# Zeros and ones of the head set by GpSimd instead of VectorE, and another order of all engines: linear attention and softmax attention in one program on one core

## The chip, the core and the metric

The kernel runs on one NeuronCore of a Trainium2 chip. A core has five engines with instruction streams of their own: TensorE (PE, matrix products into PSUM), VectorE (DVE), ScalarE (ACT), GpSimd (POOL) and SyncE (SP, which here only issues DMAs). They meet at semaphores alone. The metric is the device time of one execution in microseconds, the median of several runs.

## What is computed

Two attention blocks of the same size (S = 2048, D = 512, 32 heads of 16 columns) with inputs of their own; the results stand side by side.

```python
def _A_ref(x, wqkv, wo):                      # linear attention
    q, k, v = ...                             # (x @ wqkv), 32 heads of Dh = 16
    phi = lambda t: jnp.where(t > 0, t + 1, jnp.exp(t)) + 1e-6
    pq, pk = phi(q), phi(k)
    kv = jnp.einsum("bhsd,bhse->bhde", pk, v)
    z = jnp.einsum("bhsd->bhd", pk)
    num = jnp.einsum("bhqd,bhde->bhqe", pq, kv)
    den = jnp.einsum("bhqd,bhd->bhq", pq, z)[..., None] + 1e-6
    return (num / den) @ wo                   # heads side by side
def _B_ref(x, wqkv, wo):                      # softmax attention
    scores = jnp.einsum("bhqd,bhkd->bhqk", q, k) * Dh ** -0.5
    p = _softmax(scores, axis=-1)
    return jnp.einsum("bhqk,bhkd->bhqd", p, v) @ wo
return jnp.concatenate([a, b], axis=-1)
```

## The kernel before

**The long work is block B's softmax.** A score block is 128 keys by 512 queries of one head (L923, 32 rows of the array, so that up to four blocks of different heads run side by side). There are 32 units (four groups of eight heads, four query chunks, even and odd heads), and each holds 64 blocks: 2048 in all. A block becomes exponentials in one of two ways. ScalarE reads two or three neighbouring score banks of pS and writes float16 into PT (L1135, 128x1024 or 128x1536, counted here as a two-block or three-block exponential); PT has 25 places. Or VectorE turns one bank (of pD, or the spare fifth bank of pS) into the bits of a float16 by a scaled conversion to int16 in DI (L1039), and GpSimd adds two constants to those bits (L1219), which gives two shifted copies; the weighted sum of the three stands for the exponential. In place of GpSimd, VectorE can do the two shifts itself (L1190), where the order says so. A block of ScalarE then costs TensorE one product with the values, pPV<-PT,VV (L1293), one of VectorE three, pPV<-DI,VX and twice pPV<-DI,VV.

**The end of a unit.** All products of a unit gather in one PSUM bank, pPV. When the last is done, VectorE transposes the bank (L1322), takes reciprocals of the sums (L1331) and writes the scaled rows to OT (L1327). Until L1327 has read it, no product of the next unit can start: the bank is closed.

**Beside it** run block B's projections (L630 and L729 into pD or pS, evicted by VectorE; L671 writes K rows to KR, from where DMAs spread them to KM), the whole of block A (L630 with xTa and Wa, L745 to L748 for phi, L795, L819, L831) and the output products (L630 and L1347, evicted at L616).

**The head** loads x and the weights, builds an identity matrix on VectorE (L504 to L511), transposes the third and fourth x tile on TensorE (L1426), copies them to xTb (L616: one by VectorE, one by ScalarE) and computes the first K and Q (L1438, evicted at L1448, L1450 and L1452), so that the first scores can start before the whole of x is there. In the same stretch VectorE sets the ones in VV (L536, L538), which make a column of sums, and the zeros of the second half of KM (L540, eight pieces), which is first read with the second group of heads. GpSimd sets identf, BMk and VNa's ones (L497 to L543).

**What sets the order.** Nothing is scheduled on the chip. While the program is built, a planner with a clock of its own picks the next instruction for each engine from those that are ready; a record of readers and writers adds the semaphores. Each row of the table SEG holds, from one planned time on (every 12 us), 27 numbers that the planner uses: how far VectorE and GpSimd may lag, how many products make a batch, how many banks a job may hold, ties and their random seed. Another table gives another order of the same work.

Of the kernel before, what the change touches and what calls it, by code (L numbers as in the profile page):

```python
# [238 lines left out]
def bass_concat_heads__linear_attn_block__softmax_full_mha__prompt_kernel(nc, A_x, A_wqkv, A_wo, B_x, B_wqkv, B_wo, out):  # L239
# [130 lines left out]
    sch = Sched()  # L370
    es = contextlib.ExitStack()
    with es:
# [14 lines left out]
        KM = sb("KM", [128, 2, 2, S], BF)  # L387
        VV = sb("VV", [128, 2, 4, 33 * 17], BF)
# [150 lines left out]
        for r_, e_, sc_ in zeros:  # L539
            sch.add("dve", lambda e, r_=r_, e_=e_, sc_=sc_: e.memset(KM[:, r_, e_, sc_ * 512:(sc_ + 1) * 512], 0.0), writes=km_keys(r_, e_, sc_))  # L540
# [1193 lines left out]
```

## Time and profile before

| | |
|---|---|
| median of 3 runs | 650.66 us (649.93 to 652.45) |
| the profiled execution | 650.58 us, span 648.7 us |
| first exponential starts | 10.33 us |
| last exponential ends | 640.90 us |
| granted TensorE clock, mean | 0.997 |

The profiled execution is 0.08 us under the median. In the rows of the trace, a group has its line, engine, operation, tiles (written <- read), shapes and count; then its busy time, the mean of one in ns, and the idle time of the engine just before with what ended it. A row of the timeline begins with start and duration in us and may hold several instructions (xcount). A row of a stretch (from:to) has its length, then busy time and instructions of PE, PEld (weight loads), DVE, ACT and POOL, the granted clock as a share of full speed, the share of the DMA engines and GB/s. A row of the waits tells who waited for whom: us in total, times, longest.

### The profile page before, as it was taken

The page shows a single profiled execution, that of the slowest core. Times are in us where ns is not written, and L with a number is a line of the kernel's source. Part 1 is how long each engine was busy: PE and PEld are TensorE (multiplying, and loading weights), DVE is VectorE, ACT ScalarE, POOL GpSimd, SP SyncE. Part 2 cuts the span into 40 slices and gives each one's busy share as a digit, 9 for nine tenths or more (in the row PEclk, how much of TensorE's full clock was granted, in tenths as well). Part 3 has the DMA queues.
Part 4 walks back from the last instruction along what each step waited for, and adds up shares of the span by engine and source line. Part 5 has one row for each costly group of instructions (what it writes and reads, how often), then busy time and mean ns, then how long its engine had stood idle before and what let it go on. Part 6 is the DMA issues. An engine that isn't in the chain of part 4 may idle for free.

```text
span 648.7 us, 19621 instructions
## 1 busy us (share of the span) xinstructions
PE 634.6 (98%) x8366; PEld 214.4 (33%) x8366; DVE 608.7 (94%) x1090; ACT 632.1 (97%) x688; POOL 430.3 (66%) x729
## 2 busy tenths in 40 slices
PE   7999999999999999999999999999999999999996
PEld 5333333333333333333333232323222232222222
DVE  7999999999999999999999999999989999988984
ACT  5999999999999999999999999999999999999995
POOL 1566777877677776667767667666777766665552
PEclk9999999999999999999999999999999999999999
DMA  9700200011010000101130111002100001101111
GB/s 210 180 3 2 42 2 18 2 42 35 2 31 6 1 11 9 36 18 35 35 82 18 35 26 27 17 8 52 43 10 18 2 11 42 41 2 42 50 43 53
DMA packets 53227, 21.75 MB, mean 34 GB/s; under 512 B 44176, under 2 KB 52624, under 8 KB 53136
## 3 DMA queue, kind: packets, MB, share of 16 engines
q1 hardware_dynamic: 51664, 19.80, 13.1%
q8 instruction: 67, 1.10, 0.7%
q10 hardware_dynamic: 1472, 0.66, 0.4%
q14 instruction: 24, 0.20, 0.1%
HBM read 4.46 MB, written 4.19 MB: 13 GB/s over the span
## 4 chain that ended last, share of the span: by engine, by line
PE 49%; ACT 41%; DVE 8%; DMA 1%; issue 1%; DVEq 0%
ACT PT L1135 40%; PE pPV L1293 19%; PE pS L923 17%; PE pD L630 5%; DVE DI L1039 4%; PE pS L630 3%; ACT EA L745 1%; PE pD L729 1%; PE pD L923 1%; PE pS L729 1%; DMA KNa<-VNa 1%; DVE pPV L1322 1%; PE pS L686 1%; DVE KNa L616 0%; DVE VNa L835 0%
## 5 line engine op out<-in xcount | busy, mean ns | idle before, releaser
L1135 ACT ACTIVATE PT<-pS 128x1024 f16<-128x1024 f32 (+1 forms) x650 | 619.2, 1105 | 4.7 <-PE pS L923 3.4
L1219 POOL INT64_ADD DI<-DI x716 | 428.1, 611 | 204.1 <-DVE DI L1039 201.8
L1039 DVE TENSOR_SCALAR DI<-pD 128x512 int16<-128x512 f32 x499 | 328.7, 681 | 19.3 <-PE pD L923 14.3
L923 PE MATMUL pS<-QT,KM 32*128 32x512 bf16 x1547 | 262.6, 385 | 4.2 <-ACT PT L1135 3.5
L1293 PE MATMUL pPV<-PT,VV 128*17 128x512 f16 x1333 | 236.6, 381 | 0.0
L1293 PE MATMUL pPV<-DI,VV 128*17 128x512 f16 x1430 | 228.7, 382 | 0.0
L923 PE MATMUL pD<-QT,KM 32*128 32x512 bf16 x501 | 175.6, 385 | 0.4 <-DVE VNa L835 0.2
L1293 PE MATMUL pPV<-DI,VX 128*17 128x512 f16 x715 | 164.0, 383 | 0.3 <-DVE OT L1327 0.3
L1039 DVE TENSOR_SCALAR DI<-pS 128x512 int16<-128x512 f32 x214 | 144.9, 677 | 1.6 <-PE pS L923 1.4
L923 PEld LDWEIGHTS pS<-QT,KM 32*128 32x128 bf16 x1547 | 66.9, 91 | 238.5 <-ACT PT L1135 189.5
L1293 PEld LDWEIGHTS pPV<-PT,VV 128*17 128x17 bf16 x1333 | 52.4, 88 | 45.3 <-issue 36.9
L1293 PEld LDWEIGHTS pPV<-DI,VV 128*17 128x17 bf16 x1430 | 51.7, 88 | 42.8 <-issue 27.9
L1293 PEld LDWEIGHTS pPV<-DI,VX 128*17 128x17 bf16 x715 | 36.3, 89 | 21.5 <-issue 14.5
L923 PEld LDWEIGHTS pD<-QT,KM 32*128 32x128 bf16 x501 | 42.0, 91 | 4.0 <-DVE DI L1039 1.3
L630 PE MATMUL pD<-Wa,xTa 128*32 128x256 bf16 x704 | 28.6, 275 | 0.4 <-DVE DI L1039 0.4
L630 PE MATMUL pD<-xTb,Wb 128*32 128x512 bf16 x336 | 27.0, 384 | 0.0
L1322 DVE STREAM_TRANSPOSE pPV<-pPV 128x512 f32<-128x512 f32 x31 | 22.3, 720 | 0.0
L630 PEld LDWEIGHTS pD<-Wa,xTa 128*32 128x32 bf16 x704 | 14.9, 95 | 11.0 <-issue 6.6
L630 PE MATMUL pD<-xTa,Wa 128*32 128x512 bf16 x192 | 15.7, 384 | 0.3 <-DVE DI L1039 0.2
L616 DVE CAST KNa<-pD 128x512 bf16<-128x512 f32 x20 | 13.6, 682 | 2.3 <-PE pD L630 1.8
L745 ACT ACTIVATE EA<-pD 128x512 bf16<-128x512 f32 x24 | 15.8, 659 | 0.0
L630 PE MATMUL pD<-Wa,KNa 128*32 128x512 bf16 x176 | 14.1, 390 | 0.8 <-DMA KNa<-VNa 0.7
(136 smaller groups left out, 341.4 us busy)
## 6 DMA issues: line engine op xcount, KB each, us to landing
out_dram<-KNa SPq DMA_DIRECT2D x31, 128.0 KB, 1.7
Wa<-in_A_wqkv_dram SPq DMA_DIRECT2D x1, 1536.0 KB, 8.4
KM<-KR SPq DMA_DIRECT2D x96, 16.0 KB, 1.8
Wb<-in_B_wqkv_dram SPq DMA_DIRECT2D x2, 384.0 KB, 5.1
Wb<-in_B_wqkv_dram SPq DMA_DIRECT2D x1, 512.0 KB, 4.8
Wa<-in_A_wo_dram SPq DMA_DIRECT2D x1, 512.0 KB, 3.9
Wa<-in_B_wo_dram SPq DMA_DIRECT2D x1, 512.0 KB, 3.8
ON<-in_B_x_dram ACTq DMA_DIRECT2D x1, 256.0 KB, 2.8
```

Of the source, the lines that this page charges most:

```text
L616: return lambda e, bk: (e.tensor_copy(out_fn(), in_fn(bk)) if lane == "dve" else e.activation(out_fn(), in_fn(bk), ACTF.Copy))
L630: ins = self.e.matmul(out_[32 * g:32 * g + 32], lhsT=lhsT[:, 32 * g:32 * g + 32], rhs=rhs, start=start, stop=stop, tile_position=(0, 32 * g))
L686: return e.matmul(f32v(bk)[:, tl * 128:(tl + 1) * 128], lhsT=xTb[:, cc, t * 128:(t + 1) * 128], rhs=xTb[:, cc, t * 128:(t + 1) * 128], sta ...
L729: return e.matmul(f32v(bk)[:, tl * 128:(tl + 1) * 128], lhsT=xTb[:, cc, t * 128:(t + 1) * 128], rhs=Wb[:, cc, 1024 + Gp * 128:1024 + Gp * ...
L745: ("act", 0.0635 + n * 0.000833, f_ev("act", lambda e, bk: e.activation(EA[:, 0:n], f32v(bk)[:, c0:c0 + n], ACTF.Exp), [], ["EA"])),
L923: return e.matmul(dst, lhsT=KM[32 * g:32 * g + 32, Gp % 2, e_, j * 128:(j + 1) * 128], rhs=QT[32 * g:32 * g + 32, Gp % 2, c * 512:(c + 1) ...
L1039: sch.add("dve", lambda e: e.tensor_scalar(DI[:, di_at(0, buf) + i * 512:di_at(0, buf) + (i + n) * 512], f32v(DBANK[b0], n * 512), ESC, EB ...
L1135: sch.add("act", lambda e: e.activation(PTf[:, p0 * 512:p0 * 512 + w], S5[:, c0:c0 + w], ACTF.Exp, scale=SC), reads=skeys(sl, len(bl)), wr ...
L1219: sch.add("pool", lambda e, v=v, word=word: e.int64_add(at64(v), at64(0), word), reads=keys, writes=[("DI", v, x) for x in best])
L1293: sch.add("pe", lambda e, g=g, j=j, c0=c0, V_=V_, r2=r2, P=P, first=first, last_=last_: e.matmul(PVb[32 * g:32 * g + 17, 0:512], lhsT=V_[: ...
L1322: sch.add("dve", lambda e: e.transpose(PVb[:, 0:512], PVb[:, 0:512]), reads=[("PV", g) for g in range(4)], writes=[("PV", g) for g in rang ...
```

## The change

There are two edits. Four memsets of VV and eight of KM move from VectorE's stream to GpSimd's, at the same place of the program, and all 54 rows but one of SEG have other numbers. The table comes from a search that keeps six partial orders and counts stretches with idle TensorE. The work is the same but for the split of the blocks: 627 two-block and 24 three-block exponentials on ScalarE instead of 617 and 33 (1326 blocks, before 1333), and 722 blocks instead of 715 on VectorE; four shifts are done by VectorE (L1190), before none.

```diff
     SEG = (
-        (0.0,0.15,4,3.0,0,0,6,2,10.0,26,2.5,7.0,1.2,2.5,2,7.0,1.5,2.5,1.5,3,1,0.3,6,0,-9.0,4,1,80),
+        (0.0,0.15,4,3.0,0,0,6,4,8.0,26,3.0,7.0,0.5,2.5,2,7.0,3.0,3,1.5,1,1,0.3,4,0,0.0,4,0.5,32),
...
-        (636.0,0.3,4,3,0,1,6,4,10.0,26,2.5,7.0,0.5,1.8,2,5.0,2.0,3,1.0,2,1,1.0,6,0,-9.0,4,0,82),
+        (636.0,0.2,5,3.0,4,1,6,2,8.0,36,3.5,9.0,0.8,1.8,2,7.0,1.5,2.5,1.0,2,1,0.3,4,10,-9.0,4,2,167),
     )
...
         for r_ in range(2):
-            sch.add("dve", lambda e, r_=r_: e.memset(
+            sch.add("pool", lambda e, r_=r_: e.memset(
                 VV[:, r_, :, :].rearrange("p t (h c) -> p t h c", c=17)[:, :, :, 16:17], 1.0), writes=[("VV1", r_)])
-            sch.add("dve", lambda e, r_=r_: e.memset(VV[:, r_, :, 544:560], 1.0), writes=[("VV1", r_)])
+            sch.add("pool", lambda e, r_=r_: e.memset(VV[:, r_, :, 544:560], 1.0), writes=[("VV1", r_)])
         for r_, e_, sc_ in zeros:
-            sch.add("dve", lambda e, r_=r_, e_=e_, sc_=sc_: e.memset(KM[:, r_, e_, sc_ * 512:(sc_ + 1) * 512], 0.0), writes=km_keys(r_, e_, sc_))
+            sch.add("pool", lambda e, r_=r_, e_=e_, sc_=sc_: e.memset(KM[:, r_, e_, sc_ * 512:(sc_ + 1) * 512], 0.0), writes=km_keys(r_, e_, sc_))
```

The first place is the head. On VectorE, the twelve memsets stood between the reduction for PAR and the copy of an x tile to xTb; as zeros of two bytes they were issued there as half as many words of four.

```order
 L515 MEMSET pPV 128x512
 L532 TENSOR_REDUCE PAR<-ZMk 128x1 x2
-L536 MEMSET VV 128x132
-L538 MEMSET VV 128x4x16
-L536 MEMSET VV 128x132
-L538 MEMSET VV 128x4x16
-L540 MEMSET KM 128x256 x8
 L616 COPY xTb<-pS 128x4x128
 L1448 TENSOR_SCALAR KM<-pS,PAR 128x128 x2
```

On GpSimd they now stand between the memset of EA and that of identf, and with 512 columns each.

```order
 L503 ISA DI<-DI 128x16
 L530 MEMSET EA 128x16
+L536 MEMSET VV 128x132
+L538 MEMSET VV 128x4x16
+L536 MEMSET VV 128x132
+L538 MEMSET VV 128x4x16
+L540 MEMSET KM 128x512 x8
 L497 MEMSET identf 128x128
 L498 AFFINE_SELECT identf<-identf 128x128
```

So VectorE's copy to xTb follows PAR at once, and GpSimd's identf, BMk and VNa come twelve instructions later.

The second place is the end of the 13th unit on VectorE, from the transpose of pPV on. Before, four instructions stand between it (L1322) and the reciprocal (L1331):

```order
L1322 STREAM_TRANSPOSE pPV<-pPV 128x512 [waits s_pe]
L1039 TENSOR_SCALAR DI<-pD 128x512
L1039 TENSOR_SCALAR DI<-pD 128x512 [waits s_pe]
L788 CAST VNa<-pS 128x4x128 [waits s_pe]
L1039 TENSOR_SCALAR DI<-pD 128x512 [waits s_pe]
L1331 RECIPROCAL ZR<-pPV 128x16
L1327 TENSOR_TENSOR OT<-pPV,ZR 128x8x2x16 [waits s_dve]
L1039 TENSOR_SCALAR DI<-pS 128x512 [waits s_pe]
L1039 TENSOR_SCALAR DI<-pD 128x512 [waits s_pe]
L1039 TENSOR_SCALAR DI<-pS 128x512 [waits s_pe]
L746 TENSOR_SCALAR EC<-EA 128x33x16 [waits s_act]
L748 SCALAR_TENSOR_TENSOR KNa<-pD,EC 128x512 [waits s_dve]
```

Now there are twelve; the transpose and the first two of them, conversions of pS and pD, stand just ahead of these rows:

```order
L671 CAST KR<-pD 128x512 [waits s_pe]
L1039 TENSOR_SCALAR DI<-pS 128x512 [waits s_pe]
L1039 TENSOR_SCALAR DI<-pD 128x512 [waits s_pe]
L659 CAST QT<-pD 128x512 [waits s_pe]
L1039 TENSOR_SCALAR DI<-pS 128x512 [waits s_pe]
L1039 TENSOR_SCALAR DI<-pD 128x512 [waits s_pe]
L659 CAST QT<-pD 128x512 [waits s_pe]
L1039 TENSOR_SCALAR DI<-pS 128x512 [waits s_pe]
L1039 TENSOR_SCALAR DI<-pD 128x512 [waits s_pe]
L671 CAST KR<-pD 128x512 [waits s_pe]
L1331 RECIPROCAL ZR<-pPV 128x16
L1327 TENSOR_TENSOR OT<-pPV,ZR 128x8x2x16 [waits s_dve]
```

Four evictions of projections (KR twice, QT twice) and eight conversions have come between. On TensorE, the same closing of the bank before; a run of pS<-QT,KM that waits for s_act fills score banks for ScalarE, and pPV<-PT,VV after s_dve is the first product of the next unit:

```order
L630 MATMUL pD<-Wa,xTa 32x256 [waits s_d11,s_dve]
L630 MATMUL pD<-Wa,xTa 32x256 x15
L923 MATMUL pS<-QT,KM 128x512 [waits s_act]
L923 MATMUL pS<-QT,KM 128x512
L923 MATMUL pS<-QT,KM 128x512 [waits s_dve]
L630 MATMUL pD<-Wa,xTa 32x256 x8
L923 MATMUL pS<-QT,KM 128x512 [waits s_act]
L923 MATMUL pS<-QT,KM 128x512
L923 MATMUL pD<-QT,KM 128x512 [waits s_dve]
L630 MATMUL pD<-Wa,xTa 32x256 x8
L1293 MATMUL pPV<-PT,VV 17x512 [waits s_dve]
L1293 MATMUL pPV<-DI,VX 17x512 x3
```

And now, from the last score group ahead of that first product on:

```order
L923 MATMUL pS<-QT,KM 128x512 [waits s_act]
L923 MATMUL pS<-QT,KM 128x512
L923 MATMUL pD<-QT,KM 128x512 [waits s_dve]
L630 MATMUL pD<-xTb,Wb 32x512 x8
L630 MATMUL pS<-Wa,xTa 32x256 [waits s_d11,s_dve]
L630 MATMUL pS<-Wa,xTa 32x256 x31
L630 MATMUL pD<-Wa,xTa 32x256 [waits s_dve]
L630 MATMUL pD<-Wa,xTa 32x256 x31
L1293 MATMUL pPV<-DI,VX 17x512 [waits s_dve]
L1293 MATMUL pPV<-DI,VX 17x512
L1293 MATMUL pPV<-PT,VV 17x512 x2
L1293 MATMUL pPV<-DI,VV 17x512
```

Two runs of 32 projection matmuls of block A (of 256 columns), and the rest of a K projection, now stand between one score group and the next, and ahead of the products of the next unit.

The third place is the end of TensorE's order. Before, after the last product of an exponential:

```order
L1293 MATMUL pPV<-PT,VV 17x512 [waits s_act]
L1293 MATMUL pPV<-PT,VV 17x512
L1347 MATMUL pS<-Wa,ON 128x512 x6
L1347 MATMUL pD<-Wa,xTb 128x512 [waits s_dve]
L1347 MATMUL pD<-Wa,xTb 128x512
L1347 MATMUL pS<-Wa,xTb 128x512 [waits s_dve]
L1347 MATMUL pS<-Wa,xTb 128x512
```

And now:

```order
L1293 MATMUL pPV<-PT,VV 17x512 [waits s_act]
L1293 MATMUL pPV<-PT,VV 17x512 x2
L1347 MATMUL pS<-Wa,ON 128x512
L1347 MATMUL pD<-Wa,ON 128x512 x3
L1347 MATMUL pS<-Wa,ON 128x512 x5
L1347 MATMUL pD<-Wa,xTb 128x512 [waits s_dve]
L1347 MATMUL pD<-Wa,xTb 128x512
L1347 MATMUL pS<-Wa,xTb 128x512 [waits s_dve]
L1347 MATMUL pS<-Wa,xTb 128x512
```

Nine output products instead of six stand between the last value product and the four that wait for VectorE's last transposes; the three others stood ahead of the last score group before.

102 rows, old and new, of the table SEG are left out of this document.

## The prediction

> **What bounds the kernel now.** I read the page first, then the stretches before, between and after the exponentials, ScalarE's waits, the groups by shape, and the timeline of the head and of the longest waits.
>
> ```profile
> PE 634.6 (98%) x8366; PEld 214.4 (33%) x8366; DVE 608.7 (94%) x1090; ACT 632.1 (97%) x688; POOL 430.3 (66%) x729
> ```
> ```profile
> 0.00:10.33 10.33, 7.81 (x71) 6.82 (x71) 7.64 (x38) 2.47 (x4) 2.11 (x13) 1.00 0.87 192
> 10.33:640.90 630.57, 623.93 (x8285) 206.66 (x8283) 597.92 (x1043) 628.53 (x682) 428.14 (x716) 1.00 0.13 30
> ```
> ```profile
> PEld pS L923 <- ACT PT L1135: 189.5, 482, 1.1
> ACT PT L1135 <- PE pS L923: 3.4, 2, 2.7
> ```
>
> In the long middle ScalarE is busy 628.53 of 630.57 us. TensorE's score matmuls stand 482 times waiting for a score bank that ScalarE has yet to read, and ScalarE waits for TensorE in rows twice. So ScalarE is the bound: the time is the start of its first exponential (10.33), its work, its waits, and a tail of 7.8 us (640.90 to 648.70).
>
> A busy row of ScalarE also holds waits, because rows overlap. The real pitch is the distance between starts:
>
> ```profile
> 565.29 5.67 ACT L1135 ACTIVATE PT<-pS 128x1024 f16<-128x1024 f32 x6
> 570.72 0.73 ACT L745 ACTIVATE EA<-pS 128x512 bf16<-128x512 f32 x1
> 571.20 7.11 ACT L1135 ACTIVATE PT<-pS 128x1024 f16<-128x1024 f32 x7
> ```
> ```profile
> L1135 ACT ACTIVATE PT<-pS 128x1024 f16<-128x1024 f32 x617 | 579.9, 1084 | 2.0 <-PE pD L923 0.9 <-PE pS L923 0.7
> L1135 ACT ACTIVATE PT<-pS 128x1536 f16<-128x1536 f32 x33 | 49.3, 1494 | 2.7 <-PE pS L923 2.7
> L1039 DVE TENSOR_SCALAR DI<-pD 128x512 int16<-128x512 f32 x497 | 326.3, 679 | 17.8 <-PE pD L923 12.8 <-PE pS L923 2.1
> L746 DVE TENSOR_SCALAR EC<-EA 128x528 bf16<-128x528 bf16 x32 | 13.4, 420 | 0.8 <-ACT EA L745 0.4
> ```
>
> Six two-block exponentials take 5.43 us, 0.905 each; an EA takes 0.48. A three-block one is longer by the difference of the means (1.494 - 1.084), so 1.315. That gives 617 x 0.905 + 33 x 1.315 + 32 x 0.48 = 617.2 us of work; the other 13.4 us of the middle are ScalarE's waits, most of them of some tens of ns. Two are large:
>
> ```profile
> 464.31:467.72 3.41, 2.73 (x25) 0.80 (x25) 3.41 (x6) 3.41 (x4) 2.21 (x5) 1.00 0.16 33
> 467.72:471.13 3.41, 3.41 (x29) 0.68 (x30) 2.49 (x6) 2.49 (x3) 2.00 (x4) 0.50 0.17 49
> ```
> ```profile
> 471.15 3.04 ACT L1135 ACTIVATE PT<-pS 128x1024 f16<-128x1024 f32 x3 [0.91 <-PE pD L923]
> 594.02 0.40 PE L630 MATMUL pD<-Wa,KNa 128*32 128x512 bf16 x4 [0.67 <-DMA KNa<-VNa]
> 594.78 1.94 ACT L1135 ACTIVATE PT<-pS 128x1024 f16<-128x1024 f32 x2 [0.71 <-PE pS L923]
> ```
>
> From 464.31 TensorE has only 25 matmuls in 3.41 us, because the pPV bank is closed while VectorE finishes a unit late. The granted clock is then 0.50 for 3.41 us, and ScalarE stands 0.91 plus two short waits, about 1.3 in all. At 594 a late transposed load costs 0.71.
>
> **The change, part by part.** First the head.
>
> ```profile
> 4.23 1.06 PE L1426 MATMUL pS<-identb,ON 128*128 128x128 bf16 x8
> 5.94 1.30 PE L1438 MATMUL pS<-xTb,Wb 128*128 128x128 bf16 x8
> 6.09 2.19 DVE L540 MEMSET KM<- 128x256 uint32 x8
> 8.19 0.36 DVE L616 COPY xTb<-pS 128x512 bf16<-128x512 bf16 x1
> 8.70 0.60 PE L1438 MATMUL pS<-xTb,Wb 128*128 128x256 bf16 x4 [1.46 <-DVE xTb L616]
> 9.34 0.43 DVE L1452 CAST QT<-pS 128x256 bf16<-128x256 f32 x1 [0.27 <-PE pS L1438]
> 9.89 0.60 PE L923 MATMUL pS<-QT,KM 32*128 32x512 bf16 x5
> 10.33 12.38 ACT L1135 ACTIVATE PT<-pS 128x1536 f16<-128x1536 f32 x12 [2.67 <-PE pS L923]
> ```
> ```profile
> 1.23 0.11 POOL L530 MEMSET EA<- 128x16 bf16 x1
> 3.28 0.29 DVE L511 TENSOR_SCALAR identb<-identf,IC 128x128 bf16<-128x128 f32 x1
> 4.23 0.20 POOL L525 MEMSET BMk<- 128x128 bf16 x1
> 18.36 1.20 POOL L1219 INT64_ADD DI<-DI  x2 [12.92 <-DVE DI L1039]
> 5.81 0.59 SPq L454 DMA_DIRECT2D Wb<-in_B_wqkv_dram  x1
> 12.16 0.62 PE L729 MATMUL pD<-Wb,xTb 128*128 128x128 bf16 x8
> Wb<-in_B_wqkv_dram SPq DMA_DIRECT2D x1, 512.0 KB, 4.8
> ```
>
> The transposes of the third and fourth x tile end at 5.29, but VectorE copies one of them only at 8.19, behind its memsets. The second Q matmuls wait for that copy (1.46). Without the memsets the copy stands behind PAR and is done by 6 us. The matmuls then follow the first Q group, whose last row ends at 5.94 + 1.30 = 7.24, and as the next row starts before one ends (four of them take 0.60), at 7.1 instead of 8.70. What follows (cast, scores, exponential) shifts with it: **-1.6 us**, the first exponential at 8.7. Behind it the next loads hold: the V weights land at 5.81 + 4.8 = 10.6, and their user moves from 12.16 to 10.56.
>
> GpSimd's price: 16 columns took 0.11, 128 took 0.20, so 512 take about 0.5; eight of them and four small ones are 5 us. Bounds: 2.7 (VectorE's 0.27 for the same bytes) and 9 us (four times the 0.20, and 1 us for each strided one). From 1.34 on that ends near 6.5, and the rest of its head near 8.5; its first shift is due at 18.36 - 1.6. Nothing waits; if the cover were gone, the upper bound would still end by 13. No DMA moves.
>
> **ScalarE's work.** There are 627 two-block and 24 three-block exponentials now: +10 x 0.905 - 9 x 1.315 = **-2.8 us**. The seven score blocks that left go to VectorE, at 0.6 each (two starts, below), beside two wide and two narrow shifts (L1190, bounded by half and twice L746's 0.42, 1.2 for the four): 5.4 us more for VectorE, and 14 more pPV matmuls (four at a time, 0.8 us) for TensorE. VectorE has 32.7 idle us in the middle, so most is covered; its lateness reaches ScalarE through a bank that comes free later. Bounds 0 and 5.4; I take **+0.5**, near the lower end, since L1039's own idle time (17.8) is a wait for TensorE.
>
> **The order.** What counts is whether TensorE has the next scores in time.
>
> ```profile
> 466.49 0.39 PE L923 MATMUL pS<-QT,KM 32*128 32x512 bf16 x3
> 466.81 0.83 PE L630 MATMUL pD<-Wa,KNa 128*32 128x512 bf16 x12
> 639.02 0.39 PE L923 MATMUL pS<-QT,KM 32*128 32x512 bf16 x2
> 619.40 21.50 ACT L1135 ACTIVATE PT<-pS 128x1536 f16<-128x1536 f32 x20
> 266.16 1.26 DVE L1039 TENSOR_SCALAR DI<-pD 128x512 int16<-128x512 f32 x2
> 267.34 0.68 DVE L788 CAST VNa<-pS 128x512 bf16<-128x512 f32 x1
> ```
>
> One place of the new order is worse than any of the old. At the end of the 13th unit VectorE has twelve instructions between the transpose of pPV and its reciprocal (four before): 12 x 0.6 = 7 us of closed bank. TensorE issues eight score groups without a pPV matmul, and after the last one eight projection matmuls, two runs of 32 with 256 columns, and eight pPV matmuls before the next scores. Its time: 0.32 to the first projection (466.49 to 466.81), 2 rounds of 0.22 (three rounds of four take 0.83, one 0.39), 16 half rounds of 0.11, and for the pPV run 0.32 + 0.22 again: 3.1 us. Its scores reach ScalarE 0.42 later (594.36 to 594.78), at 3.5. By then ScalarE has run dry: the last score group here is issued at 639.02 and its exponential ends at 640.90, so 1.7 after the issue the next could start. **+1.8 us**; bounds 0.9 (the runs overlap better) and 2.8 (VectorE's chain a microsecond behind).
>
> Against that the two large waits of before: their order is gone. Counted in rounds of 0.21 us, the four score groups there hold 7 rounds of TensorE's work, the emptiest four of the new order 9 (as some of the old order that kept their clock), so I take the clock's loss away, **-1.3**; bounds -1.3 and +1.4 (the same elsewhere). The late load I keep by half, since in the new order one such use stands four score groups behind its source: **-0.4**; bounds -0.7 and +0.7.
>
> Of the clock, TensorE: Matmul & The Clock Gate (Trainium skill, the two states) says that it halves after at least one idle window of about 3.4 us. The rows agree in the 3.41 us but not in the idleness: TensorE was busy 2.73 of 3.41. By the rule no stretch of either order would be slowed, and the sum would stay at -3.7; by the row a thinly filled stretch is enough, and the sum with one such loss would be -1.0 (+1.4 for -1.3).
>
> **The tail.** Nine output matmuls stand before the last pair, six before:
>
> ```profile
> 641.27 1.47 PE L1347 MATMUL pS<-Wa,ON 128*128 128x512 bf16 x6
> 643.06 0.60 PE L1347 MATMUL pD<-Wa,xTb 128*128 128x512 bf16 x2 [0.31 <-DVE xTb L1396]
> ```
>
> Three more at 0.21 fill the 0.31 and 0.1 to 0.2 more: **+0.1**.
>
> Sum: -1.6 - 2.8 + 0.5 + 1.8 - 1.3 - 0.4 + 0.1 = -3.7. The profiled execution took 650.58 (span 648.70 and 1.88 around it), 0.08 under the median of 650.66, so the forecast is 646.9.
>
> **Rivals.** *ScalarE never runs dry (better).* The long run of projections is hidden and neither large wait comes back: -1.6 - 2.8 - 1.3 - 0.7 = -6.4, so 644.2. For it: two old units had nine instructions at that place of VectorE's order, and neither is among the large waits. Against: the old order nowhere has the 3.1 us of work found here between two score groups.
>
> *The clock halves again*, once or twice at 1.3 to 1.4: 648.2 to 649.6. For it: the row at 467.72. Against: fuller runs.
>
> *GpSimd's memsets hold up VectorE's identity chain.* If each waits for the other, identb ends not at 3.57 but when GpSimd is through, up to 8 us; with the transposes (1.06), the first K and Q (1.30) and 1.63 from the second Q to the exponential that is 12.3 at the latest, 3.6 later than forecast: 650.5. Against: L746, from SBUF to SBUF, takes 0.42 in all its rows with GpSimd at work two thirds of the time. SBUF — State Buffer (Trainium skill, who interferes with whom) says that VectorE in a two-port mode and GpSimd lock each other out for a whole instruction; no row here shows it.
>
> *VectorE becomes the bound (slower).* If in the middle its 5.4 us are not covered, they come on top of an unchanged middle: +5.4 - 1.6 = +3.8, so 654.4. It decides where less than 5 of its 32.7 idle us can be used. For it: 94% busy. Against: its idle rows are waits for TensorE.
>
> *The order does not shift the middle*: what ScalarE saves is lost in new short waits, 649.
>
> **Numbers.** As summed 0.50 (645.2 to 648.6), better 0.19, clock 0.13, memsets 0.07, unchanged middle 0.05, VectorE 0.06. 0.5% (3.3 us) is about what a measurement of this kernel can tell from no change: faster is below 647.4. Of the first case 0.33 lies there, with the second 0.52; slower is the VectorE case, 0.06; the rest, 0.42, is the same. The range 643.4 to 650.4 leaves out VectorE's case and the ends.
>
> **What would show it.** The first exponential near 8.7; the GpSimd memsets near 0.5 each and ended by 7; 651 exponentials; a row of ScalarE idle for 1 to 2 us near 265 to 275, behind a run of L630; granted clock 1.00 throughout. The forecast is wrong if the head does not move, if VectorE's wait for TensorE vanishes, or if 0.50 stands in the clock again.

## The result, and the profile after

The changed kernel took 645.97 us (median of 5 runs, 645.90 to 646.66) beside 652.45 for the kernel before on the same chip (5 runs, 649.93 to 653.30): a ratio of 0.9912, interval 0.9888 to 0.9936. In two later comparisons, on two chips, it was 0.9946 (0.9927 to 0.9966) and 0.9919 (0.9897 to 0.9942). So it is faster by 0.5 to 0.9%. The forecast was 646.9 (643.4 to 650.4). The profiled execution took 645.92, its span is 644.19; before it was 650.58 and 648.75.

The busy times, and below them the stretches before the first exponential, between the first and the end of the last, and behind it (columns as before: length, then busy us and instructions of TensorE, its weight loads, VectorE, ScalarE and GpSimd, then clock and transfers):

```profile
PE 632.2 (98%) x8380; PEld 213.4 (33%) x8380; DVE 613.7 (95%) x1088; ACT 628.5 (98%) x689; POOL 438.7 (68%) x745
```
```profile
0.00:9.19 9.19, 6.56 (x71) 5.75 (x71) 7.42 (x26) 2.47 (x4) 7.47 (x25) 1.00 0.82 186
9.19:635.97 626.78, 622.26 (x8295) 206.35 (x8293) 603.21 (x1053) 624.97 (x683) 431.23 (x720) 1.00 0.14 31
635.97:644.20 8.23, 3.36 (x18) 1.28 (x16) 3.10 (x10) 1.09 (x2) 0.00 (x0) 0.90 0.23 71
```

The head went from 10.33 to 9.19 (-1.14), the middle from 630.57 to 626.78 (-3.79), the tail, taken to the last instruction, from 7.85 to 8.22 (+0.37): -4.56 of span. The 630.57 us of the middle held 597.92 us of VectorE work, so VectorE stood idle for 32.65; now it is 603.21 of 626.78, idle 23.57. VectorE does 5.3 us more and the stretch is 3.8 us shorter.

The exponentials by shape, which are the counts that the forecast took:

```profile
L1135 ACT ACTIVATE PT<-pS 128x1024 f16<-128x1024 f32 x627 | 586.5, 1083 | 1.5 <-PE pD L923 1.0 <-PE pS L923 0.3
L1135 ACT ACTIVATE PT<-pS 128x1536 f16<-128x1536 f32 x24 | 36.1, 1505 | 1.0 <-PE pS L923 1.0
```

The head on the timeline, first VectorE's first five identity rows before, then the rows after:

```profile
1.06 0.98 DVE L506 TENSOR_SCALAR identf<-identf 128x1 f32<-128x1 f32 x5
```
```profile
1.06 2.87 DVE L506 TENSOR_SCALAR identf<-identf 128x1 f32<-128x1 f32 x5
1.27 0.66 POOL L536 MEMSET VV<- 128x132 bf16 x1
2.88 3.99 POOL L540 MEMSET KM<- 128x512 bf16 x8
5.49 0.45 DVE L511 TENSOR_SCALAR identb<-identf,IC 128x128 bf16<-128x128 f32 x1
6.00 0.62 PE L1426 MATMUL pS<-identb,ON 128*128 128x128 bf16 x8 [1.57 <-DVE identb L511]
6.85 0.40 DVE L616 COPY xTb<-pS 128x512 bf16<-128x512 bf16 x1
6.90 1.26 PE L1438 MATMUL pS<-xTb,Wb 128*128 128x128 bf16 x12
9.19 4.62 ACT L1135 ACTIVATE PT<-pS 128x1536 f16<-128x1536 f32 x4 [1.05 <-PE pS L923]
```

Two things happened at once. VectorE's copy of the x tile no longer stands behind its memsets (8.19 before, 6.85 now). But the identity is ready only at 5.94 instead of 3.57: with GpSimd's memsets running from 1.27 to 6.87, the same five short VectorE instructions take 2.87 instead of 0.98, and TensorE stands idle for 1.57 us.

And the end of the 13th unit, where the forecast saw a new wait:

```profile
264.70 6.52 ACT L1135 ACTIVATE PT<-pS 128x1024 f16<-128x1024 f32 x7 [0.35 <-PE pS L923]
270.48 1.05 PE L630 MATMUL pS<-Wa,xTa 128*32 128x256 bf16 x32
271.35 1.05 PE L630 MATMUL pD<-Wa,xTa 128*32 128x256 bf16 x32
271.58 0.60 ACT L745 ACTIVATE EA<-pS 128x512 bf16<-128x512 f32 x1 [0.35 <-PE pS L630]
271.66 0.46 DVE L1327 TENSOR_TENSOR OT<-pPV,ZR 128x256 bf16<-128x256 f32 x1
272.22 0.38 PE L1293 MATMUL pPV<-DI,VX 128*17 128x512 f16 x2
273.19 7.45 ACT L1135 ACTIVATE PT<-pS 128x1024 f16<-128x1024 f32 x8 [1.02 <-PE pD L923]
```

ScalarE stands idle for 0.35, 0.35 and 1.02, together 1.72. The first of these waits (264.70) is ahead of the two runs of L630 with 32 matmuls, the other two (1.37) are behind them. The second run ends at 272.22 by its pace (0.87 a run), just when VectorE's multiply (to 272.12) has opened the pPV bank. Which of the two sets the wait these rows can't say.

### The profile page after: what moved, and what is told of

The parts are those of the page before. It is cut to its first block, busy times and chain, and to the rows that moved or that the text cites. A ratio compares the mean times of both kernels' runs of the same rounds, so it can differ in the third digit from the quotient of the medians.

```text
span 644.2 us, 19658 instructions
## 1 busy us (share of the span) xinstructions
PE 632.2 (98%) x8380; PEld 213.4 (33%) x8380; DVE 613.7 (95%) x1088; ACT 628.5 (98%) x689; POOL 438.7 (68%) x745
## 4 chain that ended last, share of the span: by engine, by line
ACT 48%; PE 43%; DVE 9%; issue 0%; DVEq 0%
ACT PT L1135 47%; PE pPV L1293 15%; PE pS L923 14%; PE pD L630 7%; DVE DI L1039 5%; PE pS L630 2%; ACT EA L745 1%; PE pD L729 1%; PE pD L923 1%; PE pS L729 1%; DVE identf L506 1%; DVE PQT L748 0%; DVE pPV L1322 0%; DVE VV L733 0%; PE pD L1347 0%; DVE VX L736 0%
## 5 line engine op out<-in xcount | busy, mean ns | idle before, releaser
L1039 DVE TENSOR_SCALAR DI<-pD 128x512 int16<-128x512 f32 (+1 forms) x491 | 324.0, 684 | 13.0 <-PE pD L923 9.7
L1293 PE MATMUL pPV<-DI,VV 128*17 128x512 f16 x1444 | 235.5, 381 | 0.0
L1293 PE MATMUL pPV<-DI,VX 128*17 128x512 f16 x722 | 166.1, 382 | 0.0
L1039 DVE TENSOR_SCALAR DI<-pS 128x512 int16<-128x512 f32 x228 | 154.6, 678 | 1.0 <-PE pS L923 0.5
L630 PE MATMUL pD<-Wa,xTa 128*32 128x256 bf16 x800 | 32.1, 275 | 0.1
L630 PE MATMUL pD<-xTb,Wb 128*32 128x512 bf16 x336 | 26.6, 384 | 0.5 <-DVE DI L1039 0.5
L1322 DVE STREAM_TRANSPOSE pPV<-pPV 128x512 f32<-128x512 f32 x31 | 22.3, 721 | 0.1
L630 PEld LDWEIGHTS pD<-Wa,xTa 128*32 128x32 bf16 x800 | 17.5, 96 | 11.0 <-issue 7.0
L616 DVE CAST KNa<-pD 128x512 bf16<-128x512 f32 x22 | 15.0, 682 | 2.8 <-PE pD L630 2.2
L630 PE MATMUL pD<-Wa,KNa 128*32 128x512 bf16 x208 | 16.0, 384 | 0.0
L630 PE MATMUL pD<-xTa,Wa 128*32 128x512 bf16 x176 | 15.0, 384 | 0.0
```

The costliest lines, as they stand in the source:

```text
L616: return lambda e, bk: (e.tensor_copy(out_fn(), in_fn(bk)) if lane == "dve" else e.activation(out_fn(), in_fn(bk), ACTF.Copy))
L630: ins = self.e.matmul(out_[32 * g:32 * g + 32], lhsT=lhsT[:, 32 * g:32 * g + 32], rhs=rhs, start=start, stop=stop, tile_position=(0, 32 * g))
L1039: sch.add("dve", lambda e: e.tensor_scalar(DI[:, di_at(0, buf) + i * 512:di_at(0, buf) + (i + n) * 512], f32v(DBANK[b0], n * 512), ESC, EB ...
L1293: sch.add("pe", lambda e, g=g, j=j, c0=c0, V_=V_, r2=r2, P=P, first=first, last_=last_: e.matmul(PVb[32 * g:32 * g + 17, 0:512], lhsT=V_[: ...
L1322: sch.add("dve", lambda e: e.transpose(PVb[:, 0:512], PVb[:, 0:512]), reads=[("PV", g) for g in range(4)], writes=[("PV", g) for g in rang ...
```

## The experiments

A word on the measure. Runs of one kernel differ by up to 5 us here, in good part by TensorE's clock (last section), so beside the ratios I use the three stretches of each profile: head, middle, tail. The middle of the changed kernel was 626.78, 627.14 and 627.22 in three profiles.

### The memsets and the order, each alone

Back on VectorE, with the new order:

```diff
-            sch.add("pool", lambda e, r_=r_: e.memset(
+            sch.add("dve", lambda e, r_=r_: e.memset(
 ...          (the same for the ones of L538 and the zeros of L540)
```

> The changed kernel with the twelve memsets back on VectorE; the new order stays. Theory A (the move of the memsets is worth the 1.14 us by which the first exponential came earlier, 10.33 to 9.19, and nothing else hangs on it): first exponential at 10.3, identb ready near 3.6 again, time 1.1 us above the changed kernel's 645.97, so 647.1. Rival B (the head is hidden, because the first loads or a later shortage set the pace anyway): same time as the changed kernel, 646.0, although the first exponential is later. Rival C (the order was fitted to the earlier head): more than 2 us above, 648 or more.

Measured: 647.24 (646.80 to 648.24), ratio 0.9950 (0.9931 to 0.9968). The head ends at 10.33 and the middle is that of the changed kernel:

```profile
10.33 1.45 ACT L1135 ACTIVATE PT<-pS 128x1536 f16<-128x1536 f32 x1 [2.62 <-PE pS L923]
```
```profile
10.33:637.14 626.81, 622.08 (x8294) 206.44 (x8293) 603.26 (x1053) 624.99 (x683) 431.29 (x720) 1.00 0.14 31
```

Theory A holds in the profile: the new order alone gives the whole gain of the middle (626.81), and the memsets give 1.14 in the head, 10.33 against 9.19. What they give in the time isn't shown. This median is 1.3 above the changed kernel's 645.97, but the changed kernel took 646.24 and 648.04 on two other chips (below), and in six of the nine profiles with GpSimd's memsets in this place the first exponential came at 10.47 to 11.31, later than here; the last section says why.

The other half, the old table with the memsets on GpSimd:

```diff
     SEG = (
-        (0.0,0.15,4,3.0,0,0,6,4,8.0,26,3.0,7.0,0.5,2.5,2,7.0,3.0,3,1.5,1,1,0.3,4,0,0.0,4,0.5,32),
+        (0.0,0.15,4,3.0,0,0,6,2,10.0,26,2.5,7.0,1.2,2.5,2,7.0,1.5,2.5,1.5,3,1,0.3,6,0,-9.0,4,1,80),
...
```

> The kernel before with only the twelve memsets moved to GpSimd; the old order stays. Theory A: the first exponential at 9.2 and 1.1 us less than the kernel before in the same call, ratio 0.998. The other 3.4 us of the change belong to the order. Rival B (head hidden): ratio 1.000. Rival C (the old order's loss of the clock at 467 depends on when it gets there): a ratio that the head alone cannot give, off 0.998 by more than 0.002, with another number of 0.50 windows in its trace.

Measured: 652.00 (648.29 to 653.38), ratio 1.0012 (0.9996 to 1.0028). The ratio alone would fit rival B too; the profile speaks for rival C. It has a head of 10.70, not 9.19, although VectorE's rows up to its copy at 6.85 are those of the changed kernel, and the clock is lost for two windows of 3.41 us in the stretch where the kernel before lost it for one:

```profile
463.13:466.54 3.41, 2.57 (x25) 0.76 (x22) 3.41 (x7) 3.41 (x4) 2.80 (x5) 1.00 0.00 0
466.56:469.97 3.41, 3.41 (x26) 0.70 (x26) 2.83 (x6) 2.60 (x4) 1.81 (x4) 0.50 0.22 43
469.97:473.39 3.42, 3.42 (x34) 0.72 (x30) 2.16 (x4) 2.45 (x3) 1.23 (x3) 0.50 0.12 41
```

In this profile the memsets gained nothing in the head, and the middle was 1.5 longer than before. (The two runs at a mean clock of 0.999 took 648.29 and 650.04; three such runs of before 649.10 to 649.71.)

### The memsets later on GpSimd

```diff
-        for r_ in range(2):                      (ones of VV, zeros of KM)
-            sch.add("pool", ...memset...)
         mk_ident(identf, "identf")
         band(BMk, 8, 16, "BMk")
         sch.add("pool", lambda e: e.memset(VNa[:, :, :, 128:129], 1.0), writes=["VNa1"])
+        for r_ in range(2):
+            sch.add("pool", ...memset...)
```

> The changed kernel with GpSimd's order changed: its twelve memsets stand behind its own identity, its band mask and the ones of VNa, which wait for VectorE's identity. Theory A (in the changed kernel each memset of GpSimd holds up one VectorE instruction of the identity chain, 2.4 us in all, and the gain came only from the copy of the x tile that no longer stands behind the memsets): the chain takes 0.98 us for its first five rows again instead of 2.87, identb is ready at 3.6, the first exponential at 8.2 to 8.7, time 0.5 to 1.0 us below the changed kernel, 645.0 to 645.5. Rival B (the chain is slow for another reason, such as the clock or the loads): the first five rows stay at 2.9 and the time at 646.0. Rival C (GpSimd's memsets, now 5 to 11 us, hold up the copies and the K writes of VectorE instead): first exponential at 9.2 or later, 646 or more.

Measured: 646.06 (645.60 to 646.65), ratio 0.9926 (0.9905 to 0.9948).

```profile
1.06 0.98 DVE L506 TENSOR_SCALAR identf<-identf 128x1 f32<-128x1 f32 x5
4.90 0.42 DVE L616 COPY xTb<-pS 128x512 bf16<-128x512 bf16 x1 [0.35 <-PE pS L1426]
8.58 4.62 ACT L1135 ACTIVATE PT<-pS 128x1536 f16<-128x1536 f32 x4 [1.05 <-PE pS L923]
14.74 0.83 PE L630 MATMUL pD<-xTb,Wb 128*32 128x512 bf16 x12 [0.69 <-DMA xTb<-in_B_x_dram]
```

Theory A holds for the mechanism: the chain takes 0.98 again, and the first exponential is at 8.58. The time that it said, 645.0 to 645.5, was missed: 0.6 us earlier at the start, and 0.75 given back between 12 and 24, most of it at 14.74, where the third load of x is late. That load landed at 12.4 in the changed kernel's profile and at 14.6 in this one; in the repetition below it was 14.4 here and 14.9 in the changed kernel, so it varies by itself. The repetition, with both on one chip:

> The kernel with GpSimd's memsets behind its own identity, now beside the changed kernel on one chip. So far the changed kernel's first exponential stood at 9.2 where the granted clock was full by 4.6 and at 10.5 to 11.3 where it was full only by 8.7 to 10.4; TensorE stands idle for 1.57 us in its head while VectorE's identity is held up. Theory A (that idle stretch spoils a window of the clock in some runs, and without it the clock is full by 7.9 at the latest): every run of this kernel between 645.6 and 646.9, median 646.1, and 1 us or more below the changed kernel's median on this chip. Rival B (the 2 us by which the changed kernel differed between two chips is the chip's, not the head's): both kernels with the same median and the same spread, within 0.4 us.

> The changed kernel beside the one with the late GpSimd memsets. Theory A: runs spread from 645.9 to 648.9, median 647 to 648, with the first exponential between 9.2 and 11.3 by the time at which the clock gets full. Rival B: the spread and the median of the kernel with late memsets, within 0.4 us.

Measured: 646.09 (645.84 to 646.35) with late memsets and 646.24 (645.75 to 647.38) for the changed kernel, ratios to before 0.9919 both. The 1 us of theory A was not there, and the medians are rival B's. Only one run of the changed kernel on this chip, 647.38, was late, and not by its head: its profile has the first exponential at 9.19, but a tail of 9.24 instead of 8.22, as the last store landed 4.48 behind its issue instead of 3.39. Over all runs it is another matter. The head of the changed kernel ran 41 times (in it, and in four kernels below that differ only near 270), and 22 of these runs took more than 646.9; with late memsets none of 12 did. Of the 22, 17 ran on a chip on which the late memsets did not; on the chip with both it was 5 of 12 against none of 6. Six of the 22 have a profile: in four the first exponential came at 10.47 to 11.31, in two (647.28 and 647.38) at 9.19 with a tail of 9.22 and 9.24. So the later place looks steadier, with a head of 8.58 and 8.65 in its two profiles, and isn't shown to be faster where all goes well.

### The wait at the end of the 13th unit

First half of each run left out:

```diff
+    if n in (3365, 3367, 3372, 3374):   (four of the eight steps of the two runs, by their place in the order)
+        return None
```

> The changed kernel with half of the two runs of 32 projection matmuls at the end of the 13th unit left out (16 of 32 in each, so 0.87 us less TensorE work between two score groups; that part of the linear attention's projection is not computed). In the changed kernel ScalarE stands there 0.35, then 1.02 us, and the second run ends (272.22) just when VectorE's multiply opens the pPV bank (272.12). Theory A (TensorE's 3.1 us of work between the two score groups set the wait, as in the forecast): ScalarE's waits there shrink by 0.7 to 0.9 and the time by 0.6 to 0.9, to 645.1 to 645.4. Rival B (the closed bank sets it: the next pPV matmuls cannot start before 272.1 whatever stands ahead of them): the pPV run still starts near 272.2, time within 0.2 of the changed kernel, 645.8 to 646.2.

Then the reciprocal and the multiply two evictions earlier in VectorE's order, alone and together with the half runs:

```diff
+    if 3359 <= n <= 3373: keep these; at 3373 issue L1331 and L1327 first, then the others
```

> The changed kernel with only VectorE's reciprocal and multiply of the 13th unit two evictions earlier; nothing is left out. Theory A (TensorE's work sets the wait): the second run of 32 still ends near 272.2, time 646.0, within 0.2 of the changed kernel, or up to 0.3 more because two evictions come 0.7 us later. Rival B (the closed bank sets it): pPV starts earlier, ScalarE's wait of 1.02 shrinks by 0.5 or more, time 645.3 to 645.6.

> As the kernel with half runs, and VectorE's reciprocal and multiply of the 13th unit stand two evictions earlier in its order, so the bank opens about 1.2 us earlier. Theory A (work alone): the same time as with half runs alone. Rival B (bank alone): the same as with the early reciprocal alone. If both ends coincide in the changed kernel, only this one gains: ScalarE's wait there shrinks by 0.8 to 1.0 and the time by 0.6 to 0.9, 645.1 to 645.4.

> The changed kernel again, as the measure for the three others on this chip. Theory A (no stretch of its order loses the clock): 645.9 to 646.7 in every run, mean granted clock 0.998 or more in each. Rival B (the five runs so far were lucky in the phase of the clock's windows): one run in four or more at 0.997 or less and 1.2 us above the others.

Times on this chip: changed kernel 648.04 (647.28 to 648.86), half runs 646.95, early reciprocal 647.47, both 647.43. Single runs lie between 645.93 and 648.86, while the middles of the four profiles differ by 0.24 (627.14, 627.06, 627.00 and 626.90): head and tail make the spread. The three edited kernels have heads of 10.47 to 11.31 in their profiles, the changed kernel a head of 9.19 and a tail of 9.22. So the times decide nothing. The changed kernel's own expectation (A) was missed, for all its runs were above 646.7, and rival B as well, for their clocks were 0.998 and 0.999. The rows near 272 decide. ScalarE's idle times there are 0.35, 0.34 and 1.02 in this profile of the changed kernel; the last of them, with the half runs, the early reciprocal, and both:

```profile
274.40 0.39 PE L1293 MATMUL pPV<-DI,VX 128*17 128x512 f16 x2 [0.61 <-DVE OT L1327]
275.38 1.94 ACT L1135 ACTIVATE PT<-pS 128x1024 f16<-128x1024 f32 x2 [1.38 <-PE pD L923]
```
```profile
273.49 0.78 PEld L630 LDWEIGHTS pD<-Wa,xTa 128*32 128x32 bf16 x32 [0.29 <-DVE DI L1039]
275.34 1.02 ACT L1135 ACTIVATE PT<-pS 128x1024 f16<-128x1024 f32 x1 [1.21 <-PE pD L923]
```
```profile
272.96 0.62 PE L630 MATMUL pD<-Wa,xTa 128*32 128x256 bf16 x16 [0.45 <-DVE DI L1039]
274.38 2.86 ACT L1135 ACTIVATE PT<-pS 128x1024 f16<-128x1024 f32 x3 [1.22 <-PE pD L923]
```

With less TensorE work, TensorE stands 0.61 for VectorE's multiply. With the early reciprocal VectorE's next eviction comes later by the 0.7 us of the two instructions that went ahead of it, and the second run waits for it, since it frees the bank that the run writes; with both edits TensorE stands 0.45 for it. The first 0.35 stands ahead of both runs and is there in all four; the other two are together 1.36 in the changed kernel and 1.38, 1.55 and 1.22 with the edits. So the half runs alone fit rival B, the early reciprocal alone fits theory A, and the 0.8 to 1.0 expected from both together did not come. The last step takes the second run out altogether:

> The changed kernel with VectorE's reciprocal and multiply of the 13th unit two evictions earlier, half of the first run of 32 projection matmuls there left out, and the second run left out whole with the VectorE copy that reads it (so that part of the linear attention is not computed). With half runs ScalarE's waits there did not shrink, since TensorE then stood 0.61 us for VectorE's multiply; with half runs and the early reciprocal TensorE stood 0.45 us for the eviction of the bank that the second run writes. Theory A (TensorE's two runs and VectorE's chain are equally long there, and each move only brings out the other): without the second run its wait for that bank is gone, the next scores come 0.9 to 1.0 us earlier, ScalarE's last wait there falls from 1.2 to 0.2 or 0.4. Rival B (something third, a probability buffer or the bank of the scores, holds the next scores): it stays at 1.0 or more.

```profile
273.62 1.02 ACT L1135 ACTIVATE PT<-pS 128x1024 f16<-128x1024 f32 x1 [0.21 <-PE pS L923]
275.09 2.86 ACT L1135 ACTIVATE PT<-pS 128x1024 f16<-128x1024 f32 x3 [0.45 <-PE pD L923]
634.17 1.05 PE L630 MATMUL pD<-Wa,KNa 128*32 128x512 bf16 x16 [1.26 <-DMA KNa<-VNa]
```

Theory A, for the most part: the wait falls to 0.21, but a new one of 0.45 stands one exponential later, so the place still costs 0.66, where it was 1.22 with both edits and 1.36 in the changed kernel. TensorE's two runs and VectorE's chain are about equally long there, and each edit alone brought out the other. Only taking a whole projection job away shortened the wait much; as that took work from TensorE and from VectorE, it doesn't say which of the two counted. Its time, 647.01, doesn't show it, for its head ended at 10.87 and its profile met another wait: the last transposed load landed at 634.0, 4.3 us behind its issue at 629.71; in the profile of the changed kernel beside it that took 2.4.

### More work for VectorE

```diff
+    if lane == "dve" and line == 1039 and c % 60 == 30:
+        add(lane, fn, reads, writes)      (the eviction a second time, behind the first)
```

> The changed kernel with 12 of VectorE's score evictions done twice, spread evenly over the run, the second waiting for the first: 12 x 0.68 = 8.2 us more VectorE work; nothing else differs. The measure is the length from the first exponential to the end of the last (626.8 and 627.1 in two profiles of the changed kernel), since it holds no part of the head. Theory A (VectorE's extra work in the middle is mostly hidden, as in the forecast, which took 0.5 for 5.4 us): 627.2 to 628.2. Rival B (VectorE is the bound in the middle): 634 to 635. Rival C (a late eviction always reaches ScalarE through a bank, by about half): 630 to 632.

Measured: 654.56 beside 646.24 for the changed kernel on the same chip. The middle of the changed kernel there, and of this kernel:

```profile
9.19:636.41 627.22, 622.28 (x8295) 206.38 (x8293) 603.05 (x1053) 625.23 (x683) 431.20 (x720) 1.00 0.14 31
```
```profile
10.55:644.25 633.70, 626.43 (x8295) 207.38 (x8293) 610.44 (x1065) 627.25 (x683) 431.20 (x720) 1.00 0.14 30
```

VectorE's work rose by 7.39 and the middle by 6.48, its idle time was 24.2 and is 23.3. Rival B all but holds (633.70 where it said 634 to 635): of the 7.39 us, VectorE's idle time took up 0.9. In this trace ScalarE has a new wait 2 to 5 us behind each of the twelve places, of 0.3 to 0.8 us from start to start, so the late evictions reach it one by one. The twelve were all score evictions; other work, or other places, may cost less.

### The old order's lost clock

In the kernel before, one score group is issued three times and one VectorE score block twice:

```diff
+    if n == 5850: fn = three times fn
+    if n == 5851: fn = twice fn
```

> The kernel before with one score group of the closed stretch near 465 issued three times and one VectorE score block issued twice (six more matmuls, 0.64 us of TensorE time, written to the same banks with the same values). In the kernel before the 3.41 us window from 464.31 had 25 matmuls and 2.73 us of TensorE busy, and the next window ran at 0.50. Theory A (a window that is thinly filled with matmuls costs the clock): with 31 or more matmuls in it the granted clock stays at 1.00, the waits of ScalarE at 468 to 472 go, and the time falls by 1.2 us, ratio 0.998. Rival B (the loss of the clock has nothing to do with this stretch): 0.50 stands there again, ratio 1.000 or, with the extra work, 1.001.

Measured: 650.95 (649.58 to 652.48), ratio 1.0006 (0.9992 to 1.0020). In the profile the stretch kept its clock and the middle was 628.87 instead of 630.57 (1.2 less at 468 to 480, and 0.5 less at the late load of 593). But the clock was lost in the head, after a window with TensorE busy for 1.51 us, and the first exponential came at 11.58:

```profile
5.28:8.70 3.42, 1.51 (x17) 0.92 (x15) 2.92 (x13) 0.98 (x2) 0.16 (x1) 1.00 1.09 181
8.70:12.11 3.41, 3.41 (x21) 1.68 (x25) 2.27 (x7) 0.53 (x1) 0.00 (x0) 0.50 1.14 285
462.65:466.06 3.41, 3.15 (x37) 0.94 (x29) 3.41 (x6) 3.41 (x5) 3.41 (x6) 1.00 0.11 38
```

The windows also lay elsewhere on the work in this run (462.65 and 466.06, 464.31 and 467.72 before). One profile with the clock kept is in line with theory A, while the times show no gain. This stays open.

## Why the prediction came out

- **The head, -1.6: measured -1.14 in the profiles with an early clock, and by another way.** The step "the copy stands behind PAR and is done by 6 us" failed, because PAR itself came 2.4 us later. The rival that GpSimd's memsets hold up the identity chain, 0.07 in the forecast, is what happened: identb at 5.94, inside its bound of 8. I set it aside on L746, whose 0.42 does not change beside GpSimd; L746 writes 33 blocks with gaps between them and the identity rows write densely, so that row was of another form; that this is why it isn't slowed, no run shows. SBUF — State Buffer (Trainium skill, who interferes with whom) says that a VectorE instruction in a two-port mode and a GpSimd instruction block each other for the whole instruction. The rows agree: 2.87 beside the memsets, 0.98 without them. GpSimd's price was right (0.52 to 0.60 where 0.5 was taken, 0.66 for a strided one, through at 6.87 where 6.5 was said); the rival's end, 12.3, is 12.0 by its own terms.
- **The clock in the head: no term.** The copy had waited 2.9 us behind VectorE's memsets (5.29 to 8.19), and the identity comes 2.4 later now, so about 0.5 of the 1.14 is from there. The rest fits the clock, which is full from 4.3 to 4.8 on in these profiles and was full from 6.92 on before. Where it came later still, the same head was longer than before.
- **ScalarE's work, -2.8: -2.9.** The counts came as said; real pitches in the traces are 0.903 and 1.330, so +10 x 0.903 - 9 x 1.330. (The forecast's 617.2 us of work is 617.1 by its own terms.)
- **VectorE, +0.5: the step is wrong, though nothing was lost.** "VectorE has 32.7 idle us in the middle, so most is covered": 7.39 us put into a finished order cost 6.48. That was measured in the new order alone. The new order carries 5.3 us more of VectorE's work in a middle that is 3.8 us shorter, so VectorE's idle time fell by 9.1 us (32.65 to 23.57). The forecast had no term for it: it looked for single places that are worse, and took the rest as unchanged. That it is the table's other order that removed this idle time is read from these sums; no run changed the order without the split of the blocks. ScalarE's waits beyond these pitches went from 14.05 to 13.19; with +2.1 near 270, -1.25 for the clock and -0.8 for the load, all measured from start to start, that leaves -0.9 for all other places.
- **The 13th unit, +1.8: 1.7**, at the place and behind the runs that were named: the two waits there are 1.37 of idle time, and 1.66 from start to start, since rows overlap. A third, at 264.70 (0.35, or 0.46), was not forecast. The cause is wider than said: TensorE's 3.1 us of work are one limit, VectorE's chain is the other.
- **The clock, -1.3: -1.25** in the profile. The sum rightly gave the new order no such stretch: no profile of it shows 0.50 between the first and the last exponential. But with VectorE's memsets three of its seven runs (647.92 to 648.24) had a mean clock of 0.995 or 0.996, and none of these has a profile; where they lost the clock isn't known.
- **The late load, -0.4: -0.7** of idle time (-0.8 from start to start), but the risk that was kept is real: it came back in the profile of one other kernel with this order, for 0.86 of ScalarE's time.
- **The tail, +0.1: +0.37.** The output matmuls that wait for VectorE's last transposes start 2.33 behind the end of the last exponential (638.30) instead of 2.16, and the last store lands 7.67 behind it instead of 7.37. In two other profiles of the changed kernel the tail was 9.22 and 9.24, with all but one of the last four stores landing 4.2 to 4.7 us behind their issue instead of 3.2 to 3.4; that is a larger difference than the term.

The sum was -3.7 and the span gave -4.56: the forecast was 0.5 too good for the head, 0.3 too good for the tail, and 1.6 too bad for the middle (-2.2 against -3.8), most of it the VectorE term and the small waits. That the forecast lies close owes something to these opposite errors.

## What to carry to other kernels

Before a memset is moved to an idle engine, look at what its neighbour on the same memory does in that stretch: here a later time on that engine gave the shorter head (8.6 instead of 9.2) and the steadier runs. VectorE's idle share of 4%, spread over some 180 gaps, was not room for more evictions in a finished order. So cost added work as if it were on the path, and look for what a new order takes out of the idle time. Where one wait has two limits that end within 0.1 us of each other, as here, shortening one shows little. And look at head and tail of a profile before a late run is put down to either: here late loads, late stores and a late clock each moved runs by about 1 us.

## What was not expected of the hardware

*The time follows the lost clock.* The kernel before ran 24 times beside the first experiments. By mean granted clock: 649.10 to 649.71 at 0.999 (3 runs), 650.48 to 650.83 at 0.997 (5), 652.14 to 652.65 at 0.994 (4); the other 12 lie between, at 0.998, 0.996 and 0.995. One window of 3.41 us at 0.50 takes 0.0026 off the mean clock, so these three groups look like none, one and two windows at 1.3 to 1.8 us each. That is an estimate, since most of these runs have no profile and the clock also falls in the tail; by the one profile in which that stretch kept its clock, the window cost the kernel before about 1.2. The changed kernel stayed at 0.998 or 0.999 in all of 17 runs, so part of its lead over the medians of before is this, and part of it varies with the chip and the run.

*The clock comes at different times, and the head pays for it.* In the traces the first record of full clock begins at 4.3 to 4.8 in three runs of the changed head, and the first exponential is at 9.19 in each; it begins at 8.7, 8.9, 9.2, 9.5, 10.1 and 10.4 in six other kernels with the same head, with the first exponential at 10.47, 10.55, 10.70, 10.87, 11.15 and 11.31: among these six, half a microsecond later for each microsecond. The rows show the pace: the eight transposes, and the twelve matmuls behind them, take 0.62 and 1.26 in the first kind, and in the slowest of the other

```profile
6.00 1.03 PE L1426 MATMUL pS<-identb,ON 128*128 128x128 bf16 x8 [1.56 <-DVE identb L511]
7.68 2.34 PE L1438 MATMUL pS<-xTb,Wb 128*128 128x128 bf16 x12
11.31 1.45 ACT L1135 ACTIVATE PT<-pS 128x1536 f16<-128x1536 f32 x1 [1.73 <-PE pS L923]
```

The windows, counted back from the first record of full clock in steps of 3.41 us, show what delays it. In all 14 profiles the clock became full at the end of the first window in which TensorE was busy for 2.70 us or more; windows with 2.57 or less did not make it full. TensorE's idle 1.57 us before 6.00 takes a window below that, unless the windows lie so that the 3.4 us of matmuls ahead of it fill one. Two profiles whose windows lie alike, first with GpSimd's memsets early (the kernel with the early reciprocal, full clock at 10.11), then with late ones (full clock at 6.80; before the first record the column for the clock shows 1.00 for want of a record):

```profile
3.28:6.69 3.41, 1.86 (x18) 1.60 (x17) 3.01 (x12) 0.57 (x2) 3.41 (x8) 1.00 1.29 245
```
```profile
3.39:6.80 3.41, 3.41 (x33) 3.29 (x32) 1.63 (x8) 1.04 (x3) 2.81 (x9) 1.00 1.20 246
```

TensorE: Matmul & The Clock Gate (Trainium skill, the two states) says that the window runs freely and that the change therefore comes some 500 ns earlier or later; the first these traces bear out, but here the start varied by 6 us, nearly two windows.

*Busy share does not tell which window loses the clock once it is full.* It was lost after windows with TensorE busy for 2.73, 2.57 and 1.51 of 3.41 us, and kept after this one of the changed kernel, with 1.84:

```profile
4.29:7.70 3.41, 1.84 (x28) 1.65 (x27) 3.05 (x14) 0.80 (x2) 3.18 (x10) 1.00 1.14 215
```

By the rule of an idle window in TensorE: Matmul & The Clock Gate (Trainium skill, the two states) none of the three should have lost it. The number of matmuls doesn't tell them apart either: 25, 25 and 17 in the three, but 28 here, and 20 in a window of the kernel before that kept the clock (6.92 to 10.33, busy for 1.95). Nor did a busy window always bring the clock back: with the old order and GpSimd's memsets, TensorE was busy for all of 466.56 to 469.97 at 0.50, and the next window was at 0.50 too. What is counted instead stays open.
